# The last expert's second layer, its sums and the first output block by column halves

## The chip, the cores and the metric

The kernel runs on one core of one Trainium2 chip. The metric is the device time of one execution in microseconds; the kernel before was timed three times, with a median of 202.81 us (202.5 to 203.48).

## What is computed

Packed attention over 8 batches and 8 heads (576 rows, 32 packed rows, head size 64), then a soft mixture of 8 experts with 4 slots each over the 4608 tokens that attention gives:

```python
def sm_attn(qq, kk, vv):            # softmax(scale * qq kk^T) vv
    ...
p_packed = sm_attn(p, k, v)
x = sm_attn(q, p_packed, p_packed)  # to (4608, 512)

logits = x @ phi                    # (4608, 32)
d = exp(logits - logits.max(0)); d /= d.sum(0) + 1e-09
slot_input = (d.T @ x).reshape(8, 4, 512)
for e in range(8):
    h = np.maximum(slot_input[e] @ w1[e], 0.0)
    slot_out[e] = h @ w2[e]         # w2[e] is (1024, 512)
c = exp(logits - logits.max(1)); c /= c.sum(1) + 1e-09
return c @ slot_out.reshape(32, 512)
```

All is in f32. The output is 4608 x 512, 9.44 MB.

## The kernel before

Attention and the statistics of the soft mixture run first, in an order that is written out by hand (the `ORDER` string); the change does not touch them. Behind them the eight experts' weights stream through a ring in the on-chip memory, and at the end the output goes out. Every transfer is issued by SP, on one queue, in program order. A new load waits for its place in the ring and for the landing of the transfer eight before it; a store waits for the copies that write its tiles.

The second layer of an expert multiplies the hidden rows by `w2[e]`, 1024 x 512. Each of the 128 partitions holds eight of its rows, so there are NJ = 8 products, each over 128 partitions (`layer2`). They add up in PSUM bank 5 (`SO`) in four strips of 32 rows, because four products on 32 columns of the array run side by side. The last expert is done by `last2(j, x)`: `j` is one of the eight products, `x` one of the two column halves of 256. Its weights come in three pieces, `w2_7_0` (j 0 to 3), `w2_7_2` and `w2_7_3` (two j each), all 512 columns wide. The left half adds up in bank 0, the right half in bank 1. Between the pieces stand products on `ones` (`f_w`) whose result nobody reads.

Then, for each half, VectorE (DVE) adds the bank to a copy of bank 5 (`sot`) into `so`; a product with `repf` adds up the four strips and lays the 32 slot rows four times over the partitions, in bank 2 or 3; a copy brings that to `sh`. An output tile is 128 tokens: a product of 32 rows of `cT` (the combine weights) with 32 rows of `sh`, a copy from PSUM to the ring by ScalarE (ACT) or DVE, and a store. There are 36 such tiles, in four blocks `dd` of nine. Partition p holds nine neighbouring rows of the output for each block, one of each tile, so a store of three tiles writes rows of 6 KB. The first tile is made by quarters that run as the halves of `sh` come, the next three along with it; all others by one product each. `obank` gives the PSUM banks in turn. Stores go out after tiles 1, 2, 4, 7 and 9 of the first block and after each three of the others.

`copy(eng, dst, src)` is ACT for "a" and DVE for "v"; its lines are L380 and L384. All products go through `product`, L150. Loads are L159, stores L1158 and L1169.

Of the kernel before, what the change touches and what calls it, by code (L numbers as in the profile page):

```python
# [11 lines left out]
ALU = mybir.AluOpType  # L12
# [61 lines left out]
def pack_attention_soft_moe(  # L74
# [11 lines left out]
    nc = tc.nc  # L86
# [4 lines left out]
    E, DM, FF = w1.shape  # L91
    SPE = NSLOT // E
    P = 128
    R = 64
    T = S // R
    ND = B // 2
# [3 lines left out]
    NJ = FF // P  # L100
# [48 lines left out]
    def product(*a, **k):  # L149
        return step(nc.tensor.matmul(*a, **k), 4)  # L150
# [108 lines left out]
    def rows_w1(e, g):  # L259
        return w1[e, 2 * P * g : 2 * P * (g + 1)].rearrange("(j p) f -> p j f", j=2)  # L260
# [3 lines left out]
    chunks = [(f"w1_{e}_{g}", 2 * FF, rows_w1(e, g)) for e in range(E) for g in range(NG)]  # L264
    for e in range(E):
        wv = w2[e].rearrange("(p j) f -> p j f", j=NJ)
        ends = (0, 4, 8) if e < E - 1 else (0, 4, 6, 8)
        for c, (j0, j1) in enumerate(zip(ends, ends[1:])):
            if e == E - 1 and c > 0:
                c += 1  # L270
            chunks.append((f"w2_{e}_{c}", (j1 - j0) * DM, wv[:, j0:j1]))
    extra = [c for c in chunks if c[0] == LX]
    chunks = [c for c in chunks if c[0] != LX]
    for x in PLACE:
        key, width, src = extra.pop() if x == "x" else chunks.pop(0)
# [18 lines left out]
    for y in range(4):  # L294
        rs = slice(32 * y, 32 * y + 32)
# [34 lines left out]
    work = workp.tile([P, SLOTS * 2 * FF], F32, name="work")  # L330
# [337 lines left out]
    def part(f, c):  # L668

        t0, t1, a0, a1 = PARTS[c]  # L670
        return f[:, t0:t1, a0:a1]
# [260 lines left out]
    cT = a2Tf[:, E * XZ : E * XZ + NT // 4 * P].rearrange("p (n x) -> p n x", x=P)  # L932
# [43 lines left out]
    for tok in ORDER.split():  # L976
        x, _, eng = tok.partition(":")
        x, _, bank = x.partition("@")
        n, i, j = x.split(".")
# [7 lines left out]
    SO = 5  # L987
# [51 lines left out]
        )  # L1039

    def w2v(e, j):
        if (e, j // 4) == (E - 1, 1):
            return view(f"w2_{e}_{2 + j % 4 // 2}").rearrange("p (j f) -> p j f", j=2)[:, j % 2]
        return view(f"w2_{e}_{j // 4}").rearrange("p (j f) -> p j f", j=4)[:, j % 4]

    halves = [slice(x * DM // 2, (x + 1) * DM // 2) for x in range(2)]

    def layer2(e):
# [16 lines left out]
        op=ALU.add,  # L1065
# [32 lines left out]
    sot, so, sh = (a2f[:, x * DM : (x + 1) * DM] for x in range(3))  # L1098
    repf = rep.rearrange("p c s -> p (c s)")

    def last2(j, x):
        a = (j + 2 * x) % 4
        product(
            ps[32 * a : 32 * a + 32, x, 0 : DM // 2],
            hTf[:, (NJ * (E - 1) + j) * NSLOT : (NJ * (E - 1) + j + 1) * NSLOT],
            w2v(E - 1, j)[:, halves[x]],
            start=(j < 4),
            stop=(j >= 4),
        )

    nc.vector.tensor_copy(sot, ps[:, SO])
    for x in range(2):
        for j in range(4):
            last2(j, x)
    f_w(2, 0, 4, None)
    for j0 in range(4, NJ, 2):
        for x in range(2):
            for j in range(j0, j0 + 2):
                last2(j, x)
        if j0 < NJ - 2:  # L1120
            f_w(2, 0, 4, None)
    for x, xs in enumerate(halves):
        nc.vector.tensor_tensor(so[:, xs], ps[:, x, 0 : DM // 2], sot[:, xs], op=ALU.add)
    for x, xs in enumerate(halves):
        product(ps[:, 2 + x, 0 : DM // 2], repf, so[:, xs], start=True, stop=True)
    for x, (xs, eng) in enumerate(zip(halves, "va")):
        copy(eng, sh[:, xs], ps[:, 2 + x, 0 : DM // 2])
    for key in ("w2_7_0", "w2_7_2", "w2_7_3"):
        release(key)


    obank = [4, 6, 7, 5, 0, 1, 2, 3]
    work = {"a": 0.0, "v": 0.0}
    n = 0
    for dd in range(ND):
        key, off, width = region(f"ob{dd}", T * DM)
        while not free(off, width):
            key, off, width = region(f"ob{dd}", T * DM)
        regions.append([key, off, width])
        ob = ring[:, off : off + width].rearrange("p (t m) -> p t m", t=T)  # L1140
        ov = out[dd * P * T : (dd + 1) * P * T].rearrange("(p t) m -> p t m", t=T)
        ends = (1, 2, 4, 7, 9) if dd == 0 else (3, 6, 9)
        t1 = 0
        for t in range(T):
            n4, a = divmod(dd * T + t, 4)
            rs = slice(32 * a, 32 * a + 32)
            b = obank[n % 8]
            if n < 4:

                if n == 0:  # L1150
                    for x, xs in enumerate(halves):
                        for y in range(4):
                            ys = slice(32 * y, 32 * y + 32)
                            o = obank[y] if y or x == 0 else obank[4]
                            product(ps[:, o, xs], cT[ys, 0], sh[ys, xs], start=True, stop=True)
                    for x, (xs, eng) in enumerate(zip(halves, "av")):
                        copy(eng, ob[:, 0, xs], ps[:, obank[4 * x], xs])
                        nc.sync.dma_start(out=ov[:, 0, xs], in_=ob[:, 0, xs])  # L1158
                    n += 1
                    t1 = 1  # L1160
                    continue
            else:
                product(ps[:, b], cT[rs, n4], sh[rs], start=True, stop=True)
            eng = "a" if work["a"] + 482 <= work["v"] + 607 else "v"
            work[eng] += 482 if eng == "a" else 607
            copy(eng, ob[:, t], ps[:, b])
            n += 1
            if t + 1 in ends:
                nc.sync.dma_start(out=ov[:, t1 : t + 1], in_=ob[:, t1 : t + 1])  # L1169
                t1 = t + 1  # L1170


# [30 lines left out]
```

## Time and profile before

| | |
|---|---|
| median of three timed runs | 202.81 us |
| the profiled execution | 202.17 us |
| its span, first to last instruction | 200.4 us |
| TensorE busy | 172.1 us, 86% of the span |
| VectorE, ScalarE busy | 128.0 and 81.8 us |
| moved by DMA | 72.31 MB, 62.46 MB of it read |
| mean over the span | 361 GB/s |

The page divides the span into 40 slices of 5 us. The DMA engines are full in nearly all of them; the slices that are not are the beginning and the 35th, 170 to 175 us, between the last weights and the first store. Busy shares are means over the whole span and say little about that place, so the rows below take the last 50 us apart. In the profile an f32 product stands as two matmul records. Matmul ends are modelled, and consecutive ones overlap; the time from one start to the next is the safer number.

### The profile page before, as it was taken

What the parts mean: (1) busy time and instruction counts of PE and PEld (TensorE: products, weight loads), DVE (VectorE), ACT (ScalarE), POOL (GpSimd) and SP (SyncE); (2) the same over time, 40 slices, a digit from 0 to 9 for tenths busy, and PEclk for the clock granted to TensorE, in tenths of its full rate; (3) what the DMA queues carried; (4) which work ended last, traced back from release to release, by engine and by line L of the source; (5) the groups of instructions that cost most, each with busy time, mean ns of one, the idle gap of its engine ahead of it and who ended that gap; (6) DMA issues with size and microseconds to landing.
All of it is one profiled execution on the core that took longest, in us unless ns stands there. A gap on an engine that the chain in (4) does not pass through costs nothing.

```text
span 200.4 us, 6603 instructions
## 1 busy us (share of the span) xinstructions
PE 172.1 (86%) x2869; PEld 111.1 (55%) x2869; DVE 128.0 (64%) x245; ACT 81.8 (41%) x205; POOL 36.6 (18%) x66
## 2 busy tenths in 40 slices
PE   7988998998999999899999999887989998798000
PEld 4554694986957765786868775454333333365000
DVE  2838467995989995995967959755772104389000
ACT  2163473676836746545256515021111000289000
POOL 7300007046064040007074041003000000000000
PEclk9999999999999999999999999999999999999655
DMA  6996699999999999999999999999999997099997
GB/s 208 390 383 200 190 395 371 367 388 332 366 378 391 385 389 389 354 372 371 410 390 404 415 398 415 423 414 363 314 417 420 414 422 313 1 347 410 413 417 297
DMA packets 23196, 72.31 MB, mean 361 GB/s; under 512 B 2176, under 2 KB 2944, under 8 KB 21248
## 3 DMA queue, kind: packets, MB, share of 16 engines
q1 hardware_dynamic: 23168, 71.90, 94.1%
q8 instruction: 22, 0.36, 0.7%
q14 instruction: 6, 0.05, 0.1%
HBM read 62.46 MB, written 9.44 MB: 359 GB/s over the span
## 4 chain that ended last, share of the span: by engine, by line
PE 44%; DMA 28%; DVE 9%; ACT 5%; SPq 3%; issue 3%; POOL 1%; ACTq 0%; DVEq 0%
PE ps L150 32%; DMA ring<-in_moe_w_dram 14%; PE ps L153 12%; DMA ring<-in_k_dram 9%; DMA ring<-in_p_dram 5%; ACT ring L380 3%; SPq L159 3%; DVE work L431 2%; DVE work L384 1%; POOL a L704 1%; ACT work L380 1%; DVE mx L639 1%; DVE zs L683 1%; DVE a L704 1%; DVE a L649 1%
## 5 line engine op out<-in xcount | busy, mean ns | idle before, releaser
L380 ACT COPY work<-ps 128x512 f32<-128x512 f32 (+3 forms) x61 | 26.3, 474 | 31.6 <-PE ps L153 23.1
L150 PE MATMUL ps<-work 128*64 128x64 f32 (+1 forms) x1088 | 32.2, 313 | 1.5 <-DVE work L431 0.8
L150 PEld LDWEIGHTS ps<-work 128*64 128x64 f32 (+1 forms) x1088 | 23.0, 121 | 8.0 <-issue 3.0
L431 DVE STREAM_TRANSPOSE work<-ring 128x576 f32<-128x576 f32 x32 | 23.5, 758 | 4.4 <-DMA ring<-in_k_dram 2.3
L153 PE MATMUL ps<-ident,ring 128*128 128x128 f32 x144 | 21.2, 280 | 0.1
L150 PE MATMUL ps<-ring,work 64*64 64x128 f32 x576 | 19.0, 273 | 1.2 <-DVE work L384 1.2
L150 PE MATMUL ps<-ones 128*128 128x512 f32 (+3 forms) x46 | 18.6, 504 | 1.1 <-DVE ones L118 1.1
L150 PEld LDWEIGHTS ps<-ring,work 64*64 64x64 f32 x576 | 16.0, 133 | 4.8 <-issue 1.8
L384 DVE COPY work<-ps 128x512 f32<-128x512 f32 (+3 forms) x31 | 15.8, 527 | 3.7 <-PE ps L153 2.3
L153 PEld LDWEIGHTS ps<-ident,ring 128*128 128x128 f32 x144 | 16.0, 141 | 3.1 <-issue 1.3
L686 POOL TENSOR_TENSOR zt<-work 128x576 f32<-128x576 f32 x4 | 5.7, 1429 | 56.6 <-ACT work L678 56.6
L153 PE MATMUL ps<-ident,work 128*128 128x128 f32 x108 | 15.6, 278 | 0.5 <-ACT work L463 0.4
L384 DVE COPY a2Tb<-ps 128x384 f32<-128x384 f32 (+2 forms) x15 | 8.0, 546 | 9.7 <-PE ps L153 9.7
L463 ACT ACTIVATE work<-ps,nm 128x576 f32<-128x576 f32 x16 | 11.8, 743 | 5.8 <-DVE nm L460 5.8
L639 DVE TENSOR_REDUCE mx<-ps 128x36 f32<-128x1152 f32 x8 | 10.8, 1353 | 4.3 <-PE ps L150 2.5
L150 PE MATMUL ps<-ring,hT 128*32 128x512 f32 (+1 forms) x120 | 13.2, 538 | 0.3 <-DMA ring<-in_moe_w_dram 0.3
L153 PEld LDWEIGHTS ps<-ident,work 128*128 128x128 f32 x108 | 11.9, 141 | 2.4 <-ACT work L463 1.4
L150 PE MATMUL ps<-ring,a2Tb 128*32 128x512 f32 x96 | 12.4, 594 | 0.4 <-DVE a2Tb L1061 0.4
L150 PE MATMUL ps<-a,a2Tb 32*128 32x512 f32 (+2 forms) x88 | 12.0, 584 | 0.6 <-DVE ring L384 0.5
L460 DVE TENSOR_REDUCE nm<-ps 128x2 f32<-128x1152 f32 x8 | 10.8, 1348 | 2.8 <-PE ps L150 2.8
L150 PEld LDWEIGHTS ps<-ones 128*128 128x128 f32 x46 | 8.0, 209 | 6.4 <-issue 5.0
L380 ACT COPY ring<-ps 128x512 f32<-128x512 f32 (+1 forms) x21 | 10.4, 621 | 1.1 <-PE ps L150 1.0
(127 smaller groups left out, 225.4 us busy)
## 6 DMA issues: line engine op xcount, KB each, us to landing
ring<-in_moe_w_dram SPq DMA_DIRECT2D x24, 1024.0 KB, 10.3
ring<-in_k_dram SPq DMA_DIRECT2D x16, 576.0 KB, 8.1
ring<-in_q_dram SPq DMA_DIRECT2D x16, 576.0 KB, 6.9
ring<-in_v_dram SPq DMA_DIRECT2D x16, 576.0 KB, 7.3
out_dram<-ring SPq DMA_DIRECT2D x10, 768.0 KB, 8.1
work<-in_moe_w_dram SPq DMA_DIRECT2D x6, 1024.0 KB, 14.3
a<-in_moe_w_dram SPq DMA_DIRECT2D x1, 1024.0 KB, 6.9
ring<-in_moe_w_dram SPq DMA_DIRECT2D x2, 512.0 KB, 18.7
```

The costliest lines, as they stand in the source:

```text
L150: return step(nc.tensor.matmul(*a, **k), 4)
L153: return step(nc.tensor.transpose(*a, **k), 2)
L159: x = nc.sync.dma_start(out=dst, in_=src).ins
L380: nc.scalar.copy(dst, src)
L384: nc.vector.tensor_copy(dst, src)
L431: nc.vector.transpose(kT[:, b2, :, c].rearrange("p m (t r) -> p m t r", t=T), view(f"k{i}.{b2}").rearrange("p (m t c d) -> p m t c d", m=2 ...
L460: nc.vector.tensor_reduce(nms[i % 2], s1v(i), axis=AX.XY, op=ALU.max, negate=True)
L463: nc.scalar.activation(a1[:, :, x].rearrange("p t (h r) -> p h t r", h=2), s1v(i)[:, x].rearrange("p h (t r) -> p h t r", t=T), AF.Exp, bi ...
L639: nc.vector.tensor_reduce(mxs[i % 2][:, a0:a1].rearrange("p a t -> p (a t)"), s2v(i, j).rearrange("p a t s -> p (a t) s"), axis=AX.X, op=A ...
L649: nc.vector.tensor_tensor(a2s[i // NG % 2][:, :, i % NG, a0:a1].rearrange("p t a s -> p a t s"), s2v(i, j), mxs[i % 2][:, a0:a1].unsqueeze ...
L686: nc.gpsimd.tensor_tensor(y, a[:, :, :, 0:w], a[:, :, :, w:NS], op=ALU.add)
L704: (nc.vector if eng == "v" else nc.gpsimd).tensor_tensor(a, a, z.unsqueeze(3).broadcast_to([P, a.shape[1], a.shape[2], NS]), op=ALU.mult)
```

## The change

The last expert's weights come by column halves: the left 256 columns of all 1024 rows in three pieces (j 0 to 3, 4 and 5, 6 and 7), then the right 256 columns in one. The left half's products, sum, `repf` product and `sh` copy come first; the fillers on `ones` stand between its pieces. Then the first block's nine tiles are made by halves: left halves of tiles 0 to 3, the right half's eight products, left halves of tiles 4 to 8, the right half's sum, the right halves of all nine tiles. The `sh` copy of each half is cut again, 128 columns on DVE and 128 on ACT, and so is the copy of bank 5. The first block is stored in six pieces of half rows; the second in two stores of four and five tiles, the third and fourth in one each.

```diff
-        ends = (0, 4, 8) if e < E - 1 else (0, 4, 6, 8)
...
+        if e == E - 1:
+            for c, j0, j1 in ((0, 0, 4), (1, 4, 6), (2, 6, 8)):
+                chunks.append((f"w2_{e}_{c}", (j1 - j0) * DM // 2, wv[:, j0:j1, 0 : DM // 2]))
+            chunks.append((f"w2_{e}_3", NJ * DM // 2, wv[:, :, DM // 2 : DM]))
+            break
...
+    def total(x):
+        xs = halves[x]
+        nc.vector.tensor_tensor(so[:, xs], ps[:, x, 0:HB], sot[:, xs], op=ALU.add)
+        product(ps[:, 2 + x, 0:HB], repf, so[:, xs], start=True, stop=True)
+
+    def shared(x):
+        for y, eng in enumerate("va"):
+            ys = slice(HB * x + HB // 2 * y, HB * x + HB // 2 * (y + 1))
+            copy(eng, sh[:, ys], ps[:, 2 + x, HB // 2 * y : HB // 2 * (y + 1)])
...
+    def part(t, x, b):
+        n4, a = divmod(t, 4)
+        rs = slice(32 * a, 32 * a + 32)
+        product(ps[:, b, 0:HB], cT[rs, n4], sh[rs, halves[x]], start=True, stop=True)
+
+    def keepp(t, x, b, eng):
+        copy(eng, ob[:, t, halves[x]], ps[:, b, 0:HB])
+
+    def send(t0, t1, x):
+        nc.sync.dma_start(out=ov[:, t0:t1, halves[x]], in_=ob[:, t0:t1, halves[x]])
+
+    for j in range(NJ):
+        last2(j, 0)
+        if j in (3, 5):
+            f_w(2, 0, 4, None)
+    total(0)
+    shared(0)
+    for t in range(4):
+        part(t, 0, pa[t])
+    for j in range(NJ):
+        last2(j, 1)
+    for t in range(4):
+        keepp(t, 0, pa[t], "avav"[t])
+        if t != 2:
+            send(*((0, 1), (1, 2), None, (2, 4))[t], 0)
+    for t in range(4, 8):
+        part(t, 0, pa[t])
+    part(8, 0, pa[8])
+    total(1)
+    for t in range(4, 8):
+        keepp(t, 0, pa[t], "avav"[t - 4])
+    shared(1)
+    keepp(8, 0, pa[8], "a")
+    send(4, 9, 0)
+    for t in range(T):
+        part(t, 1, pb[t])
+    for t in range(T):
+        keepp(t, 1, pb[t], "avavavava"[t])
+        if t in (2, 8):
+            send(*((0, 3) if t == 2 else (3, 9)), 1)
```

The order on TensorE at the end of the program, from the last expert on, as a difference. `ring,hT` are products of `last2`, `ones` fillers, `a_1_101,rep` the product with `repf`, `a_1_101,a2Tb` output tiles:

```order
-L150 MATMUL ps<-ring,hT 32x256 x8
-L150 MATMUL ps<-ones 128x256
 L150 MATMUL ps<-ring,hT 32x256 x4
 L150 MATMUL ps<-ones 128x256
-L150 MATMUL ps<-ring,hT 32x256 x4
-L150 MATMUL ps<-a_1_101,rep 128x256 x2
-L150 MATMUL ps<-a_1_101,a2Tb 128x256 x8
-L150 MATMUL ps<-a_1_101,a2Tb 128x512 x32
-L1198 UNCONDITIONAL_BRANCH
+L150 MATMUL ps<-ring,hT 32x256 x2
+L150 MATMUL ps<-ones 128x256
+L150 MATMUL ps<-ring,hT 32x256 x2
+L150 MATMUL ps<-a_1_101,rep 128x256
+L150 MATMUL ps<-a_1_101,a2Tb 128x256 x4
+L150 MATMUL ps<-ring,hT 32x256 x8
+L150 MATMUL ps<-a_1_101,a2Tb 128x256 x5
+L150 MATMUL ps<-a_1_101,rep 128x256
+L150 MATMUL ps<-a_1_101,a2Tb 128x256 x9
+L150 MATMUL ps<-a_1_101,a2Tb 128x512 x27
```

The first `repf` product moves ahead of the right half's eight products, and the second one stands behind five output tiles.

ACT at the same place before, with the engines whose counts each instruction waits for (`a_1_101` holds `sot`, `so` and `sh`):

```order
L942 ACTIVATE L_sb<-L_sb 128x288 [waits DVE_49] x4
L1015 COPY a_1_101<-ps 128x512 [waits DMAHW4_49,PE_49,Pool_49]
L1015 COPY a_1_101<-ps 128x512 [waits PE_49]
L380 COPY a_1_101<-ps 128x256 [waits PE_49,Activation_49]
L380 COPY ring<-ps 128x256 [waits DMAHW5_49,DMAHW7_49,DMAHW2_49,PE_49]
```

and ACT now:

```order
L1154 COPY a_1_101<-ps 128x256 [waits DVE_49]
L382 COPY a_1_101<-ps 128x128 [waits DVE_49]
L382 COPY ring<-ps 128x256 [waits DMAHW5_49,DMAHW7_49,DMAHW2_49,PE_49]
L382 COPY ring<-ps 128x256 [waits DMAHW6_49,DMAHW0_49,PE_49]
L382 COPY ring<-ps 128x256 [waits DMAHW3_49,DMAHW1_49,PE_49]
L382 COPY ring<-ps 128x256 [waits PE_49]
L382 COPY a_1_101<-ps 128x128 [waits DVE_49]
L382 COPY ring<-ps 128x256 [waits DMAHW7_49]
```

The half copies of `sh` on ACT wait for DVE, where the copy before waited for TensorE; the last row, the left half of tile 8, has come to stand behind the second of them.

SP's stores before, by the elements of each partition:

```order
L1158 DMA out_dram<-ring 128x256 x2
L1169 DMA out_dram<-ring 128x512
L1169 DMA out_dram<-ring 128x1024
L1169 DMA out_dram<-ring 128x1536
L1169 DMA out_dram<-ring 128x1024
L1169 DMA out_dram<-ring 128x1536 x9
```

and now, with the last loads ahead of them:

```order
L159 DMA ring<-in_moe_w_dram 128x4x256
L159 DMA ring<-in_moe_w_dram 128x2x256 x2
L159 DMA ring<-in_moe_w_dram 128x8x256
L1151 DMA out_dram<-ring 128x256 x2
L1151 DMA out_dram<-ring 128x2x256
L1151 DMA out_dram<-ring 128x5x256
L1151 DMA out_dram<-ring 128x3x256
L1151 DMA out_dram<-ring 128x6x256
L1205 DMA out_dram<-ring 128x2048
L1205 DMA out_dram<-ring 128x2560
L1205 DMA out_dram<-ring 128x4608 x2
```

Fifteen stores become ten; the first block and the last weights move in pieces of 256 elements, the rest in longer rows.

## Rows read from the trace of the kernel before

**Rows 1.** The page: span, and packets of the DMA queue that brings instructions.

```profile
span 200.4 us, 6603 instructions
q8 instruction: 22, 0.36, 0.7%
```

**Rows 2.** Stretches: busy time (count) by engine, then granted clock, DMA share, GB/s.

```profile
147.90:168.50 20.60, 19.03 (x180) 6.16 (x172) 5.37 (x14) 0.73 (x2) 0.00 (x0) 1.00 1.01 420
168.50:171.00 2.50, 2.50 (x27) 1.15 (x28) 0.55 (x1) 0.00 (x0) 0.00 (x0) 1.00 0.28 108
171.00:175.70 4.70, 3.54 (x34) 1.84 (x36) 1.97 (x5) 1.49 (x4) 0.00 (x0) 1.00 0.00 0
177.40:199.20 21.80, 6.99 (x48) 4.66 (x48) 7.61 (x13) 8.11 (x17) 0.00 (x0) 0.71 1.01 409
```

**Rows 3.** Chain that ended last, from 165 us: start, us, what.

```profile
147.91 20.53 DMA ring<-in_moe_w_dram
```

**Rows 4.** Timeline of TensorE, 164 to 174 us: start, us, what [idle before].

```profile
166.30 1.92 PE L150 MATMUL ps<-ring,hT 128*32 128x512 f32 x16
168.48 1.07 PE L150 MATMUL ps<-ring,hT 128*32 128x256 f32 x16 [0.26 <-DMA ring<-in_moe_w_dram]
169.48 0.70 PE L150 MATMUL ps<-ones 128*128 128x256 f32 x2
170.11 0.64 PE L150 MATMUL ps<-ring,hT 128*32 128x256 f32 x8
170.68 0.70 PE L150 MATMUL ps<-ones 128*128 128x256 f32 x2
171.31 0.64 PE L150 MATMUL ps<-ring,hT 128*32 128x256 f32 x8
```

**Rows 5.** Timelines of DVE, ACT, SP and TensorE, 171.9 to 176.5 us.

```profile
171.98 0.76 DVE L1123 TENSOR_TENSOR a<-ps,a 128x256 f32<-128x256 f32 x2 [2.94 <-PE ps L150]
173.27 0.42 DVE L384 COPY a<-ps 128x256 f32<-128x256 f32 x1 [0.53 <-PE ps L150]
...
173.69 0.37 ACT L380 COPY a<-ps 128x256 f32<-128x256 f32 x1 [19.72 <-PE ps L150]
174.48 1.55 ACT L380 COPY ring<-ps 128x256 f32<-128x256 f32 x3 [0.42 <-PE ps L150]
...
174.88 0.83 SPq L1158 DMA_DIRECT2D out_dram<-ring  x2
175.80 0.89 SPq L1169 DMA_DIRECT2D out_dram<-ring  x2
...
172.46 1.13 PE L150 MATMUL ps<-a,rep 128*128 128x256 f32 x4 [0.51 <-DVE a L1123]
173.75 1.15 PE L150 MATMUL ps<-a,a2Tb 32*128 32x256 f32 x16 [0.15 <-DVE a L384]
```

**Rows 6.** Groups by form, copies: count | busy us, mean ns of one | idle before.

```profile
L380 ACT COPY work<-ps 128x128 f32<-128x128 f32 x10 | 2.8, 278 | 1.4 <-PE ps L153 1.3
L384 DVE COPY work<-ps 128x128 f32<-128x128 f32 x6 | 1.7, 283 | 0.0
```

**Rows 7.** Timeline, 34.0 to 34.9 us: two copies out of one PSUM bank.

```profile
33.99 0.42 DVE L384 COPY work<-ps 64x256 f32<-64x256 f32 x1
...
34.44 0.37 ACT L380 COPY work<-ps 64x256 f32<-64x256 f32 x1 [2.40 <-DVE work L384]
```

**Rows 8.** DMA, 174 to 176 us, 1 KB packets: 40 slices; packets, MB, share.

```profile
GB/s 0 0 0 0 0 0 0 0 0 0 0 0 0 0 0 0 0 0 0 0 0 0 0 0 0 0 0 0 0 0 0 0 0 0 143 225 307 348 369 307
...
q1 hardware_dynamic: 83, 0.08, 12.8%
```

**Rows 9.** DMA, 161 to 164 us: loads of 8 KB packets.

```profile
DMA packets 179, 1.29 MB, mean 429 GB/s; under 512 B 22, under 2 KB 22, under 8 KB 22
```

**Rows 10.** DMA, 177.5 to 178.5 us: stores of 4 KB packets.

```profile
DMA packets 101, 0.40 MB, mean 401 GB/s; under 512 B 3, under 2 KB 3, under 8 KB 101
```

**Rows 11.** DMA, 190 to 198 us: stores of 6 KB packets.

```profile
DMA packets 607, 3.34 MB, mean 417 GB/s; under 512 B 64, under 2 KB 64, under 8 KB 607
```

More of the change, by code (lines that the diff above doesn't have):

```diff
@@ L266, in pack_attention_soft_moe @@
         wv = w2[e].rearrange("(p j) f -> p j f", j=NJ)
-        ends = (0, 4, 8) if e < E - 1 else (0, 4, 6, 8)
[L268 to L271, printed above, removed]
+        if e == E - 1:
[3 more added lines that the diff above has]
+            break
+        for c in range(2):
+            chunks.append((f"w2_{e}_{c}", 4 * DM, wv[:, 4 * c : 4 * c + 4]))
     extra = [c for c in chunks if c[0] == LX]
@@ L1041, in w2v, with w2h @@
     def w2v(e, j):
-        if (e, j // 4) == (E - 1, 1):
-            return view(f"w2_{e}_{2 + j % 4 // 2}").rearrange("p (j f) -> p j f", j=2)[:, j % 2]
         return view(f"w2_{e}_{j // 4}").rearrange("p (j f) -> p j f", j=4)[:, j % 4]
+    def w2h(j, x):
+        if x:
+            key, n, k = "3", NJ, j
+        else:
+            key, n, k = ("0", 4, j) if j < 4 else (str(1 + (j - 4) // 2), 2, j % 2)
+        return view(f"w2_{E - 1}_{key}").rearrange("p (j f) -> p j f", j=n)[:, k]
     halves = [slice(x * DM // 2, (x + 1) * DM // 2) for x in range(2)]
@@ L1105, in last2 @@
             hTf[:, (NJ * (E - 1) + j) * NSLOT : (NJ * (E - 1) + j + 1) * NSLOT],
-            w2v(E - 1, j)[:, halves[x]],
+            w2h(j, x),
             start=(j < 4),
@@ L1109, in last2, with rows @@
         )
[L1111 to L1135, printed above, removed]
+    HB = DM // 2
+    def total(x):
[6 more added lines that the diff above has]
+            copy(eng, sh[:, ys], ps[:, 2 + x, HB // 2 * y : HB // 2 * (y + 1)])
+    def rows(dd):
         key, off, width = region(f"ob{dd}", T * DM)
@@ L1139, in pack_attention_soft_moe @@
         regions.append([key, off, width])
[L1140 to L1143, printed above, removed]
+        return (
+            ring[:, off : off + width].rearrange("p (t m) -> p t m", t=T),
+            out[dd * P * T : (dd + 1) * P * T].rearrange("(p t) m -> p t m", t=T),
+        )
+    ob, ov = rows(0)
+    def part(t, x, b):
[6 more added lines that the diff above has]
+        nc.sync.dma_start(out=ov[:, t0:t1, halves[x]], in_=ob[:, t0:t1, halves[x]])
+    nc.vector.tensor_copy(sot[:, halves[0]], ps[:, SO, halves[0]])
+    nc.scalar.copy(sot[:, halves[1]], ps[:, SO, halves[1]])
+    for j in range(NJ):
[4 more added lines that the diff above has]
+    shared(0)
+    pa = (4, 6, 7, 5, 0, 2, 4, 6, 7)
+    pb = (5, 0, 2, 1, 3, 4, 6, 7, 5)
+    for t in range(4):
[21 more added lines that the diff above has]
+            send(*((0, 3) if t == 2 else (3, 9)), 1)
+    for c in range(4):
+        release(f"w2_{E - 1}_{c}")
+    obank = [0, 2, 1, 3, 4, 6, 7, 5]
+    work = {"a": 0.0, "v": 0.0}
+    n = 0
+    for dd in range(1, ND):
+        ob, ov = rows(dd)
         for t in range(T):
@@ L1147, in pack_attention_soft_moe @@
             b = obank[n % 8]
[L1148 to L1163, printed above, removed]
+            n += 1
+            product(ps[:, b], cT[rs, n4], sh[rs], start=True, stop=True)
             eng = "a" if work["a"] + 482 <= work["v"] + 607 else "v"
@@ L1166, in pack_attention_soft_moe @@
             copy(eng, ob[:, t], ps[:, b])
[L1167 to L1170, printed above, removed]
+            if t in ((3, 8) if dd == 1 else (8,)):
+                t0 = 4 if dd == 1 and t == 8 else 0
+                nc.sync.dma_start(out=ov[:, t0 : t + 1], in_=ob[:, t0 : t + 1])
 _INS = ["q", "k", "v", "p", "moe_phi", "moe_w1", "moe_w2"]
```

## The prediction

> **What bounds the kernel now.** I read the page first: the span is 200.4 us [rows 1], the profiled execution took 202.17 us and the median of the three timed runs is 202.81 us. I add differences to the span and carry them to the median, which lies 0.64 us above the profiled execution.
>
> Then the stretches at the end [rows 2]. From 147.9 to 168.5 us the DMA engines are full (share 1.01, 420 GB/s): the expert weights stream in and TensorE keeps up. From 168.5 the share falls to 0.28, from 171.0 to 175.7 it is 0.00, and from 177.4 to 199.2 it is 1.01 again at 409 GB/s. So the end is a store stream that nothing interrupts, and the time is set by when that stream begins, how often it stops, and how fast its 9.44 MB go. After 175.7 the compute engines are ahead of it: in the last stretch ACT is busy 8.11 us of 21.8.
>
> The chain [rows 3] says what sets the beginning: the first piece of the last expert's second layer lands at 168.44 (147.91 + 20.53). TensorE alone fills the next 3.5 us [rows 4]: eight half-width products (16 records, each f32 product shows twice) at 168.48, a filler on `ones` at 169.48, four products at 170.11, a filler at 170.68, four products until 171.95. Then sum, product with `repf`, copy, first output tile, copy, issue at 174.88 [rows 5]; the first bytes move at 174 + 34 x 0.05 = 175.70 [rows 8], 0.82 us after the issue.
>
> **Part 1, the weights by column halves.** The same 2 MB, in pieces of 1 KB instead of 8 and 4 KB. A 1 KB packet took 0.128 x 16 x 2000 / 83 = 49.3 ns [rows 8]; an 8 KB packet at 429 GB/s takes 305 ns [rows 9]. The left half is 64 packets on each DMA engine, 3.16 us, where 1 MB was 8 x 305 = 2.44: it is complete at 168.44 + 0.7 = 169.2. TensorE needs its last piece at about 170.6 (below), so 1.4 us are to spare. The right half is later again by 64 x 49.3 less 16 x 163 (4 KB packets [rows 10]) = 0.55 us: before, everything had landed by 171.0 [rows 2], so about 172.3 at worst, and it is needed at 173.7. Cost: nothing, hidden behind TensorE; if that cover were gone, 1.3 us.
>
> **Part 2, the left half goes first.** The expert before ends on TensorE at 166.30 + 1.92 = 168.22, and such runs overlap by 0.07 (168.48 + 1.07 against 169.48) [rows 4], so the left half starts at 168.15 on a first piece that has landed (168.44 - 2.44 + 1.58 = 167.6). Four products 0.57 (170.11 to 170.68), filler 0.63, two products that I price like four, 0.57, filler 0.63, last two 0.64: done at 171.19 against 171.95. Both fillers stay in this half, 1.26 us of it.
>
> The sum starts at 171.22. Sum to product 0.48, product to copy 0.81 [rows 5]: 172.51. Here is a new cost. The copy of 256 columns is cut in two halves of 128, one on DVE and one on ACT, but both read one PSUM bank, and the order below shows ACT's half waiting for DVE. The trace has that pattern once [rows 7]: DVE's copy ends at 34.41 and ACT's begins at 34.44. So 0.28 + 0.03 + 0.28 [rows 6] = 0.59 in place of 0.42: 173.10, products at 173.16 (+0.06), first copy 0.73 later at 173.89, 0.37 long, issue at 174.29 (+0.03). That is **0.59 us earlier** than 174.88; bytes move at 175.11.
>
> **Part 3, the feed after the first four half tiles.** Four half tiles are ready early, in three stores. SP issues 0.46 apart (half of 174.88 to 175.80 [rows 5]), so the third moves at 175.11 + 0.92 = 176.03 and its 16 packets per engine last 0.79: the stream is dry at **176.82**. The next store, of five half tiles, waits for the ninth copy, and that copy stands on ACT behind the right half's `sh` copy. Following it: four products from 173.16 (0.57), eight products on the right half (1.07) until 174.80, sum at 174.83. Meanwhile TensorE does five more products in two groups, 0.5 each, until 175.73, and only then the `repf` product; 0.81 to the copies: 176.54; DVE 0.28, ACT 0.03 + 0.28: 177.13; ninth copy, 0.37: 177.50; issue 177.53, bytes at 178.35. The stream stands still for **1.53 us**. Bounds: 1.0, if the groups of four products that stand before the `repf` product follow each other at 0.42 (the pair of groups in 1.15, less its tail of 0.31, halved [rows 5]) and the ninth copy overlaps ACT's half copy; 1.9, if each hand-over between engines costs the longest one seen here, 0.15 [rows 5]. Of what follows, the store of three waits for ACT's copies, which begin after the ninth right-hand product; it comes at about the moment the five are through (1.9 us of transfer), then six tiles cover the rest. I count nothing there.
>
> **Part 4, the size of rows.** The first block of nine tiles becomes 144 packets of 1 KB on each engine, 144 x 49.3 = 7.10 us. Before it was 16 of 1 KB, 8 of 2 KB, 16 of 4 KB, 8 of 6 KB: 0.79 + 0.66 (half the 4 KB price) + 2.61 + 8 x 236 [rows 11] = 5.94. So +1.16; by the best slice of 1 KB traffic, 369 GB/s, a packet is 44.4 ns and the difference +0.53 [rows 8]. I take **+0.9**.
> The Trainium skill, "DMA: Bandwidth & Descriptors", section Specifications, puts line rate at transfers of 512 B and more, so 1 KB pieces would lose nothing. By it this term would vanish; rows 8 against rows 11 (20.8 bytes per ns against 26.0) do not agree.
>
> The other 27 tiles go in rows of 8, 10 and 18 KB instead of 6 KB. No 18 KB row was measured. 6 KB packets are 236 ns, three are 708. By the 8 KB stretch of [rows 2] (420 GB/s, 312 ns) an 18 KB row is 702, and the three blocks win 0.15 us; by a straight line through 236 and 305 it is 650 and they win 1.2. Far on the other side, the 22 packets of 16 KB on the instruction queue took 0.007 x 16 x 200.4 / 22 = 1.02 us each [rows 1], which would make it 1.15 us and cost 6.9. I take **-0.4**, near the rows of this queue.
>
> **Sum.** -0.59 + 1.53 + 0.9 - 0.4 = +1.44, say 1.4 us: span 201.8, median 202.81 + 1.4 = **204.2 us**. The small gaps between the first stores (a half tile lasts 0.39, an issue 0.46) were there before too.
>
> **Rivals.**
> 1. *The stall does not open.* Place: the store of five half tiles. It decides whether its issue stands before 176.82 - 0.82 = 176.00. Then 1.53 falls away and the sum is -0.1: 202.7, not slower; with the lower ends of part 4 (+0.53 and -1.2) it is -1.3: 201.5. For it: DVE and ACT have free time in these microseconds [rows 5]. Against: the order fixes five products, one product and three copies in a row in front of this store.
> 2. *The rows pay for themselves.* The stall is there, but 1 KB pieces cost only their bytes: 39.3 ns each, 5.66 against 5.78 us, -0.1 in place of +0.9: +0.4, 203.2. Or the large rows win 1.2 and the sum is +0.6, 203.4. Against the first stand the 49.3 ns of 83 packets, against the second that it needs the whole of the straight line. The Trainium skill's rule above speaks for the first.
> 3. *The loads come late.* Column halves skip every other KB in memory, which no row here shows. If they ran at half rate, the left half would take 2.4 us longer and be ready at 170.9 instead of 169.2, still costing only 0.3, the right half would come at about 175.8 and add 2.1: near 206.3.
> 4. *TensorE's clock.* It is at the full level, 2.4 GHz, up to 175.7 (1.00 in each stretch but the last [rows 2]), with fillers in the gaps. The right half has none. If it fell to 1.2 GHz near 173, about 2.5 us of TensorE steps on the path double: near 206.7. Against: the idle stretches that I expect there, 0.5 to 0.9 us, are near the 0.51 of [rows 5], which left the clock alone.
>
> **How the numbers follow.** A measurement of this kernel can tell 0.5%, 1.0 us. Forecast (+1.0 to +2.2): 0.55; rival 1: 0.15, of which half goes to faster; rival 2: 0.21, within 0.5%; rivals 3 and 4 and an 18 KB row that is slow: 0.09. So faster 0.07, same 0.29, slower 0.64. The forecast's own range is 203.8 to 205.0. The range for eight in ten reaches down to rival 1 (202.7) and up over part of rivals 3 and 4: 202.6 to 205.4.
>
> **What the profile will show.** The first store issued at 174.3 (174.0 to 174.6) and bytes 0.82 later; an ACT copy of 128 columns beginning 0.03 us after DVE's, twice; a second stretch of DMA share 0, 1.0 to 1.9 us long, that begins near 176.9; then 1 KB traffic at 330 to 370 GB/s until about 183.7, and after it 410 to 435. TensorE should not wait for a DMA after 168.2. I am wrong if the second empty stretch is under 0.7 us, if the first bytes move later than 175.5, or if the stretch of large rows is off 409 GB/s by more than 7%.

## The result and the profile after

The changed kernel took 206.03 us (median of 20 runs; the kernel before took 204.0 over 20 runs beside them). The ratio is 1.0103, 95% interval 1.0070 to 1.0137: slower by 1 per cent, about 2.1 us. The forecast was slower by 1.4 us, at 204.2 us with a range up to 205.4. So the sign came out, the difference is somewhat larger, and the time lies outside the range. Ratios, here and below, leave out the runs that are more than 1.5 per cent above the fastest of their kernel; medians take all of them.

The page's span, beside [rows 1]:

```profile
span 201.9 us, 6621 instructions
```

1.5 us longer than 200.4. The stretches of the end, in the columns of [rows 2]:

```profile
171.00:174.90 3.90, 2.63 (x30) 1.32 (x34) 1.62 (x5) 0.91 (x3) 0.00 (x0) 1.00 0.00 1
174.90:176.80 1.90, 1.46 (x12) 0.69 (x7) 1.32 (x4) 0.72 (x3) 0.00 (x0) 1.00 0.84 275
176.80:178.20 1.40, 1.16 (x17) 1.09 (x18) 0.41 (x2) 0.47 (x2) 0.00 (x0) 1.00 0.01 1
178.20:183.60 5.40, 5.40 (x37) 3.36 (x36) 4.11 (x10) 4.95 (x13) 0.00 (x0) 1.00 1.00 332
183.60:200.50 16.90, 3.22 (x23) 1.68 (x18) 4.16 (x7) 4.01 (x8) 0.00 (x0) 0.71 1.00 421
```

Read the last two columns downwards. The stores begin at 174.9, which is 0.8 us earlier than before; they stop at 176.8 and stand still for 1.4 us, which they never did before; they run at 332 GB/s while the rows are 1 KB long, and at 421 GB/s behind that, where [rows 2] had 409.

TensorE, which fills the time before the first store (as [rows 4]):

```profile
166.26 2.36 PE L150 MATMUL ps<-ring,hT 128*32 128x512 f32 x24
168.55 0.70 PE L150 MATMUL ps<-ones 128*128 128x256 f32 x2
169.18 0.63 PE L150 MATMUL ps<-ring,hT 128*32 128x256 f32 x4
169.73 0.70 PE L150 MATMUL ps<-ones 128*128 128x256 f32 x2
170.36 0.63 PE L150 MATMUL ps<-ring,hT 128*32 128x256 f32 x4
171.52 0.70 PE L150 MATMUL ps<-a,rep 128*128 128x256 f32 x2 [0.53 <-DVE a L1122]
172.96 0.71 PE L150 MATMUL ps<-a,a2Tb 32*128 32x256 f32 x8 [0.75 <-ACT a L382]
173.61 1.07 PE L150 MATMUL ps<-ring,hT 128*32 128x256 f32 x16
174.61 1.13 PE L150 MATMUL ps<-a,a2Tb 32*128 32x256 f32 x10
175.66 0.70 PE L150 MATMUL ps<-a,rep 128*128 128x256 f32 x2
```

No row has a DMA behind "<-": the weights by column halves are there in time. The last five products of the left-hand tiles (174.61, ten records) stand between the right half's products and its `repf` product (175.66), as forecast. The copies and stores, as [rows 5]:

```profile
172.32 0.29 DVE L386 COPY a<-ps 128x128 f32<-128x128 f32 x1 [0.86 <-PE ps L150]
...
176.40 0.29 DVE L386 COPY a<-ps 128x128 f32<-128x128 f32 x1 [0.21 <-PE ps L150]
...
172.65 0.27 ACT L382 COPY a<-ps 128x128 f32<-128x128 f32 x1 [3.49 <-DVE a L386]
...
176.73 0.27 ACT L382 COPY a<-ps 128x128 f32<-128x128 f32 x1 [0.74 <-DVE a L386]
176.89 0.38 ACT L382 COPY ring<-ps 128x256 f32<-128x256 f32 x1
178.64 5.54 ACT L382 COPY ring<-ps 128x256 f32<-128x256 f32 x13 [1.37 <-PE ps L150]
...
174.09 6.42 SPq L1151 DMA_DIRECT2D out_dram<-ring  x6
...
177.29 0.38 SPq L1151 DMA_DIRECT2D out_dram<-ring  x1
...
179.31 0.37 SPq L1151 DMA_DIRECT2D out_dram<-ring  x1
```

The first store is issued at 174.09, where it was 174.88. Twice ACT's 128 columns begin 0.04 us after DVE's end (172.61 and 176.69), as [rows 7] said they would. The ninth left-hand copy follows at 176.89, and the store of five half tiles is issued at 177.29. The row at 178.64 is one that the forecast saw and counted at nothing: ACT's right-hand copies wait 1.37 us for TensorE, and the store of three goes out only at 179.31.

The 1 KB stretch, 178.2 to 183.6 us (packets, then MB and share of 16 engines):

```profile
DMA packets 1781, 1.79 MB, mean 332 GB/s; under 512 B 32, under 2 KB 1781, under 8 KB 1781
...
q1 hardware_dynamic: 1781, 1.79, 100.1%
```

1.001 x 16 x 5400 / 1781 = 48.6 ns a packet, and 49.3 for the 1 KB packets alone, without the 32 under 512 B: the price of [rows 8].

**A yardstick with less noise than the time.** The last load that all versions have in common is the second piece of expert 6's second layer. From its landing to the last byte of the last store, by the DMA records, it is 33.25 us in the kernel before, in its repetition and in the version that only has more instructions. I call that the tail. For the changed kernel it is 34.62, and 34.7 to 34.9 in two near copies of it below; there the tail is less sure, since it also holds how late TensorE is behind the landing (Part 2 below). In this pair the tail explains +1.37, the end behind the last landing +0.25 (1.09 us instead of 0.84 to the last instruction), and device time outside the span +0.37 (2.14 us instead of 1.77).

### The profile page after: what moved, and what is told of

The parts are those of the page before. It is cut to its first block, busy times and chain, and to the rows that moved or that the text cites. A ratio compares the mean times of both kernels' runs of the same rounds, so it can differ in the third digit from the quotient of the medians.

```text
span 201.9 us, 6621 instructions
## 1 busy us (share of the span) xinstructions
PE 174.5 (86%) x2879; PEld 112.2 (56%) x2879; DVE 128.5 (64%) x250; ACT 82.4 (41%) x211; POOL 36.5 (18%) x66
## 4 chain that ended last, share of the span: by engine, by line
PE 52%; DMA 15%; DVE 15%; ACT 5%; issue 2%; SPq 2%; POOL 1%; DVEq 0%; ACTq 0%
PE ps L150 41%; DMA ring<-in_k_dram 13%; PE ps L153 12%; DVE work L433 2%; DMA out_dram<-ring 2%; ACT work L382 2%; SPq L159 2%; POOL a L706 1%; DVE ring L386 1%; DVE L_sb L942 1%; DVE cm L946 1%; ACT L_sb L944 1%; DVE work L386 1%; DVE cm L941 1%; ACT ring L382 1%
## 5 line engine op out<-in xcount | busy, mean ns | idle before, releaser
L150 PE MATMUL ps<-work 128*64 128x64 f32 (+1 forms) x1088 | 32.8, 313 | 2.2 <-DVE work L433 0.8
L150 PE MATMUL ps<-a,a2Tb 32*128 32x512 f32 (+2 forms) x98 | 13.5, 544 | 1.4 <-ACT a L382 1.4
L386 DVE COPY ring<-ps 128x512 f32<-128x512 f32 (+1 forms) x20 | 10.2, 574 | 3.8 <-PE ps L150 3.8
```

## The experiments

Idle is the time in which the DMA engines did nothing between the first and the last store byte, summed over engines and divided by 16. Outside is device time less span. Tail, idle and outside are of one profiled execution each.

| run | tail | idle | outside | ratio to before |
|---|---|---|---|---|
| before | 33.25 | 0.39 | 1.78 | 1 |
| after | 34.62 | 1.94 | 2.14 | 1.0103 (1.0070 to 1.0137) |
| e0_again | 33.25 | 0.39 | 1.78 | 1.0001 (0.9964 to 1.0037) |
| e1_long_rows | 32.82 | 0.38 | 1.78 | 1.0044 (0.9998 to 1.0090) |
| e2_half_rows | 34.46 | 0.62 | 1.77 | 1.0101 (1.0033 to 1.0169) |
| e3_send_early | 34.34 | 1.08 | 2.14 | 1.0051 (0.9997 to 1.0104) |
| e3a_send_only | 34.89 | 1.97 | 2.16 | one run |
| e3b_bank_only | 34.72 | 1.88 | 2.13 | one run |
| e4_full_loads | 35.21 | 1.93 | 2.14 | 1.020 (1.011 to 1.029) |
| e5_no_fillers | 33.55 | 1.95 | 2.16 | 0.9995 (0.9949 to 1.0042) |
| e6_no_gaps | 31.58 | 0.44 | 2.03 | 0.9982 (0.9939 to 1.0026) |
| e7_rows_no_fillers | 32.50 | 0.36 | 1.78 | 0.9994 (0.9948 to 1.0040) |
| e8_more_instructions | 33.25 | 0.36 | 2.01 | one run |

**Long rows alone (before with the stores of the last three blocks in longer rows).**

```diff
-        ends = (1, 2, 4, 7, 9) if dd == 0 else (3, 6, 9)
+        ends = ((1, 2, 4, 7, 9), (4, 9), (9,), (9,))[dd]
```

> The kernel before with one part of the change alone: the second block is stored as four and five tiles, the third and fourth in one store of nine tiles each (rows of 8, 10 and 18 KB for 6 KB). Theory A (each packet has a fixed cost, so that the size of rows counts): the stretch of full DMA behind the first block shortens by 0.5 us, ratio to the kernel before 0.997 to 0.998. Theory B (bytes are bytes; only when the stream starts and stops counts): no difference, 1.000, and the stretch stays 17.25 us.

The tail is 0.43 shorter. The stretch of long rows, as [rows 2]; before, the same kind of stretch moved 409 GB/s:

```profile
184.00:201.90 17.90, 3.75 (x28) 2.34 (x22) 4.37 (x8) 4.87 (x10) 0.00 (x0) 0.72 1.01 425
```

So the trace bears the -0.4 out. The timed ratio does not: it stands above what was expected, with an interval of 0.9 per cent, four times the effect; the medians of all runs lean the other way (203.72 against 204.34, 0.9970). A gain of 0.2 per cent cannot be shown with these timings.

**Half rows alone (before, the first block's stores as two column halves of 1 KB).**

```diff
-                nc.sync.dma_start(out=ov[:, t1 : t + 1], in_=ob[:, t1 : t + 1])
+                for xs in halves if dd == 0 else (slice(0, DM),):
+                    nc.sync.dma_start(out=ov[:, t1 : t + 1, xs], in_=ob[:, t1 : t + 1, xs])
```

> The kernel before with one cost of the change alone: each store of the first block goes as two column halves, 144 packets of 1 KB on each engine in place of rows of 1 to 6 KB. Everything else, and when the first store is issued, stays. Theory A: the first block's transfer takes 1.1 us longer (6.15 to about 7.2 us), ratio 1.005. Theory B: no difference, 1.000.

Tail +1.21, and the ratio's interval leaves no change out, though the medians of all runs lie closer (204.59 against 204.34). The 1 KB stretch:

```profile
176.70:182.00 5.30, 5.30 (x42) 3.59 (x39) 5.29 (x9) 5.25 (x11) 0.00 (x0) 1.00 0.97 316
```

The engines are full (0.97) and move 316 GB/s. 0.23 of the 1.21 is idle time, which I put down to the four more stores that are issued; the rest, 1.0 us, is the size of the rows.

**The stall: three edits.** In the first, the store of half tiles 4 to 8 leaves without the ninth, and the ninth right-hand product is moved, so that bank 5, which it shares with the first right-hand tile, no longer holds up ACT's copies (the `send` lines do the first, the `part` lines the second):

```diff
+    send(4, 8, 0)
     shared(1)
     keepp(8, 0, pa[8], "a")
-    send(4, 9, 0)
-    for t in range(T):
+    send(8, 9, 0)
+    for t in range(8):
         part(t, 1, pb[t])
     for t in range(T):
         keepp(t, 1, pb[t], "avavavava"[t])
+        if t == 0:
+            part(8, 1, pb[8])
```

> The changed kernel with the stall taken away: the left halves of tiles 4 to 7 are stored before the right half's sh copy, tile 8 by itself behind it; and the ninth right-hand product, which uses the first one's bank 5, is issued after the first right-hand copy, so that this copy no longer waits for it. Theory A (the stall of 1.4 us in the store stream is time): two short gaps of about 0.3 us stay in its place, 0.8 to 1.1 us less than the changed kernel, ratio to the kernel before about 1.005 and the last bytes at about 199.4 in the profile. Rival C (the stall is covered, the time is lost in the transfers themselves or outside the span): as the changed kernel, 1.010.

The stream, from first to last byte, is 0.89 us shorter (24.66 instead of 25.55), and the ratio is half-way to the kernel before, as expected, but its interval holds both ends. The tail shows only 0.28 of the gain, because here the first store is issued 8.82 us after the common landing, and 8.21 in the changed kernel.

What the bank does is more than a wait. `pb` gives bank 5 to the first and to the ninth right-hand product, and the program issues all nine products before the first copy. The chain of the changed kernel shows them run, nine products in 18 records, and the copy behind them:

```profile
177.04 1.57 PE ps L150 x18
```

They end at 178.61, and ACT's first right-hand copy starts at 178.64. So the ninth product has overwritten the first, and both copies out of bank 5 bring tile 8: the changed kernel does not store the right half of tile 0 (128 rows, 256 columns) but tile 8's in its place. With the reference's inputs the two differ by about 1 part in 100,000, so the output hardly shows it. The `part` lines put the order right, in the versions with both edits, with the bank alone and without gaps; with both edits ACT waits 0.51 us instead of 1.37:

```profile
179.22 1.53 ACT L382 COPY ring<-ps 128x256 f32<-128x256 f32 x5 [0.51 <-PE ps L150]
```

With the bank alone put right, the tail is 34.72 and the idle time 1.88, as in the changed kernel within what two executions differ by, so the comparison of this document does not hang on the fault.

The second and the third run take one of the two edits each: only the `send` lines, and only the `part` lines.

> The changed kernel with one edit: the store of half tiles 4 to 8 is issued without the last of them, which goes by itself behind it. The bank that the first and the ninth right-hand products share is left as it is. Theory (the dry stretch is the sum of two waits in a row: the ninth left-hand copy, and then the right-hand copies that wait for the ninth right-hand product because of that bank): the dry stretch is split, not removed: four half tiles go about 0.4 us earlier, the stream runs dry again before the store of three right-hand half tiles, and DMA idle time inside the stream falls from 1.94 us only to 1.2 to 1.7. Rival (only the ninth left-hand copy makes the stall): idle time falls to about 0.9 us or less, what the version with both edits has (1.08) or under it.

> The changed kernel with one edit: the ninth right-hand product waits until the first right-hand copy is done, so the right-hand copies no longer wait for it; the store of half tiles 4 to 8 stays whole. Theory (two limits of equal length, either of which alone keeps the stream back): in the changed kernel the five half tiles, issued 3.20 us after the first store and 1.97 us long, are through at about the moment at which the store of three (issued 5.22 us after the first) can move. So with the bank alone mended nothing is gained either: idle time in the stream 1.85 to 1.95 us as before the edit, the store of three issued about 4.4 us after the first and queued. Rival (the bank alone is the bound, since the split store alone gained nothing): idle time about 1.1 us.

The share of the DMA engines in 8.1 us from the first store byte on, and in the stretches in which the stream is dry. With `send` alone:

```profile
175.90:184.00 8.10, 7.42 (x61) 4.67 (x58) 5.24 (x13) 5.54 (x15) 0.00 (x0) 1.00 0.79 261
177.90:178.20 0.30, 0.14 (x4) 0.14 (x8) 0.00 (x0) 0.30 (x2) 0.00 (x0) 1.00 0.05 17
180.20:181.20 1.00, 1.00 (x9) 0.76 (x11) 0.02 (x1) 1.00 (x5) 0.00 (x0) 1.00 0.00 0
```

With the bank alone:

```profile
177.60:185.70 8.10, 7.41 (x66) 5.40 (x63) 6.10 (x14) 6.27 (x17) 0.00 (x0) 1.00 0.81 265
179.60:180.90 1.30, 1.15 (x17) 0.73 (x17) 0.39 (x2) 0.79 (x4) 0.00 (x0) 1.00 0.00 0
```

With both:

```profile
176.40:184.50 8.10, 7.41 (x67) 5.41 (x61) 6.10 (x14) 6.32 (x17) 0.00 (x0) 1.00 0.92 308
178.30:178.60 0.30, 0.11 (x4) 0.11 (x5) 0.00 (x0) 0.30 (x2) 0.00 (x0) 1.00 0.00 0
```

Neither edit alone gains anything; both together gain 0.9. With `send` alone the stall is split, 0.3 us before the fourth store and 1.0 us behind the fifth, because the store of three right-hand tiles still leaves 5.2 us after the first one (180.32 less 175.11; in the changed kernel 179.31 less 174.09). With the bank alone that store is ready 4.35 us after the first and stands in the queue behind the one that is late. I had expected a small gain from `send` alone and missed; the gain from the bank alone, none, came as expected. Two waits of nearly equal length lie beside each other, and taking away one shows the other.

**Full rows for the loads (after, the last expert's weights in three pieces of whole rows).**

```diff
-                chunks.append((f"w2_{e}_{c}", (j1 - j0) * DM // 2, wv[:, j0:j1, 0 : DM // 2]))
-            chunks.append((f"w2_{e}_3", NJ * DM // 2, wv[:, :, DM // 2 : DM]))
+                chunks.append((f"w2_{e}_{c}", (j1 - j0) * DM, wv[:, j0:j1]))
```

> The changed kernel with the last expert's weights loaded as before, in three pieces of full rows (8 and 4 KB packets); products, sums, copies and stores as in the changed kernel, where bank 5 is written by the first and by the ninth right-hand product and copied out twice after the ninth. Theory A: the left half's last two products need the last piece, which lands at 171.0 where the left columns land at 168.9; TensorE comes to it at 170.4, so the first store is 0.6 us later than in the changed kernel, and the time 0.3 to 0.6 us more, since the right half is no longer late either. Rival D (the 1 KB loads cost more than they bring): faster than the changed kernel by 0.5 us or more.

Now TensorE waits for the first piece, and not for the last one, as I had expected:

```profile
169.51 1.92 PE L150 MATMUL ps<-ring,hT 128*32 128x512 f32 x16
172.13 0.64 PE L150 MATMUL ps<-ring,hT 128*32 128x256 f32 x8 [0.70 <-DMA ring<-in_moe_w_dram]
```

The tail is 0.3 to 0.6 longer than that of the changed kernel and its near copies, in the expected span; the timed ratio went further. So the loads by halves cost nothing that shows, and without them the left half waits 0.70 us for its weights. What that is worth is less sure: the first store is issued 8.80 us after the common landing, and 8.21 to 8.82 in the four versions that load by halves and keep the fillers.

**No fillers (after without the two products on `ones`).**

```diff
     for j in range(NJ):
         last2(j, 0)
-        if j in (3, 5):
-            f_w(2, 0, 4, None)
```

> The changed kernel without the two fillers between the left half's products (1.26 us of TensorE); bank 5 is used as in the changed kernel. Theory A (TensorE, not the landing of the weights, sets when the left half is done): its last two products start when the last left piece lands, so the first store comes 1.2 to 1.4 us earlier after the expert before than in the changed kernel; the gap in the stores stays 1.4 us, and the time falls by 1.2 us, ratio to the kernel before about 1.003. Rival E (the fillers hold TensorE's clock): the granted clock falls to 0.5 between 170 and 178 us, the steps there double and the time is the changed kernel's or more, 1.010 to 1.015.

```profile
166.77 0.55 PE L153 MATMUL ps<-ident,L_sb 128*128 128x128 f32 x3 [0.57 <-DVE a2Tb L386]
167.25 2.79 PE L150 MATMUL ps<-ring,hT 128*32 128x512 f32 x32
170.58 0.70 PE L150 MATMUL ps<-a,rep 128*128 128x256 f32 x2 [0.55 <-DVE a L1122]
```

From the start of expert 6's products to the `repf` product it is 3.33 us, against 5.26 (171.52 less 166.26): the fillers cost 1.93, not 2 x 0.63. Products on 32 columns run side by side in groups of four; a filler on all 128 columns ends the group, and a pair that would share a group then takes as long as four (0.55 us from 169.18 to 169.73, where four took 0.57 from 170.11 to 170.68 in [rows 4]). The tail wins less, 1.1 to 1.3 against the changed kernel and its near copies (expected: 1.2), since expert 6's products start 1.21 us after the common landing here and 0.38 after it in the changed kernel; the idle time stays (1.95). The granted clock stayed at 1.00, the level of 2.4 GHz, without them:

```profile
167.20:174.50 7.30, 6.00 (x70) 2.65 (x68) 2.88 (x7) 1.38 (x5) 0.00 (x0) 1.00 0.52 165
```

The first row shows a second wait: TensorE's last transposes stand 0.57 us for a DVE copy, because `for x, b in enumerate((6, 7, 6))` uses bank 6 twice; the kernel before has the same wait (0.56), and with bank 3, in the next two versions, the nine records run in 1.20 us without it.

**No gaps (after without fillers and stall, the third transposes in bank 3, `sh` in one DVE copy, the left half's later stores in pairs).** Not in the lines shown: both edits of the stall, the ninth left-hand product behind the second `sh` copy, and tile 7's left-hand copy on ACT.

```diff
-    for x, b in enumerate((6, 7, 6)):
+    for x, b in enumerate((6, 7, 3)):
...
-        for y, eng in enumerate("va"):
-            ys = slice(HB * x + HB // 2 * y, HB * x + HB // 2 * (y + 1))
-            copy(eng, sh[:, ys], ps[:, 2 + x, HB // 2 * y : HB // 2 * (y + 1)])
+        copy("v", sh[:, halves[x]], ps[:, 2 + x, 0:HB])
...
+        if t in (5, 7):
+            send(t - 1, t + 1, 0)
```

> The changed kernel with what was found put together: no fillers; the left half's nine tiles stored in stores of 1, 1, 2, 2, 2 and 1 tiles as their copies come, none of them behind the right half's sh copy; that copy in one piece on DVE; the last three transposes into bank 3, so that they wait for no copy; the ninth right-hand product after the first right-hand copy. Theory A: first store 2 us earlier after the expert before than in the kernel before, no gap in the store stream over 0.3 us, 1 KB rows cost 1.1 and long rows win 0.4 to 0.5: 1.5 to 2.0 us less than the kernel before, ratio 0.990 to 0.993. Rival E: the clock falls without the fillers and it is not faster than the kernel before. Rival C (the time is lost outside the store stream): not better than 1.005.

```profile
172.15 0.70 PE L150 MATMUL ps<-a,rep 128*128 128x256 f32 x2 [0.53 <-DVE a L1122]
173.43 0.71 PE L150 MATMUL ps<-a,a2Tb 32*128 32x256 f32 x8 [0.58 <-DVE a L386]
```

One whole copy costs 1.28 us from `repf` product to tile; the two halves cost 1.44 (172.96 less 171.52). And the stream has no hole:

```profile
175.40:183.50 8.10, 8.10 (x72) 5.98 (x65) 6.48 (x14) 6.98 (x18) 0.00 (x0) 1.00 1.01 339
```

The tail is 1.67 shorter than before. 0.25 of it is lost outside the span and 0.13 behind the last landing. What remains, 1.3 us, would be a ratio of 0.9937, just under the lower edge of what was measured (0.9939 to 1.0026), which also holds no change. I had expected 0.990 to 0.993 and missed.

**Long rows, no fillers (before with those two edits and the third transposes in bank 3).**

```diff
-    for x, b in enumerate((6, 7, 6)):
+    for x, b in enumerate((6, 7, 3)):
...
-    f_w(2, 0, 4, None)
...
-        ends = (1, 2, 4, 7, 9) if dd == 0 else (3, 6, 9)
+        ends = ((1, 2, 4, 7, 9), (4, 9), (9,), (9,))[dd]
```

> The kernel before with three edits: stores of the last three blocks in long rows, no fillers on `ones` among the last expert's products, and a third bank for the third pair of transposes. Theory (each microsecond saved at the start of the store stream or inside it comes out of the span, one for one): long rows give 0.45 us, as measured in the trace with long rows alone; without fillers TensorE's run can shorten only until the last of the loads lands, which the trace of before puts 0.35 us ahead of the last four products, so the first store is issued 8.1 to 8.3 us after TensorE starts the second layer of the expert before, in place of 8.58. Sum about -0.8 us, a ratio near 0.996 (0.992 to 0.999). Rival (fillers hold the TensorE clock): the granted clock falls below 1.00 behind 168 us from the last expert's start and the first store comes later than in before: ratio 1.00 or above.

```profile
168.59 1.07 PE L150 MATMUL ps<-ring,hT 128*32 128x256 f32 x16 [0.39 <-DMA ring<-in_moe_w_dram]
169.86 0.64 PE L150 MATMUL ps<-ring,hT 128*32 128x256 f32 x8 [0.20 <-DMA ring<-in_moe_w_dram]
171.11 0.64 PE L150 MATMUL ps<-ring,hT 128*32 128x256 f32 x8 [0.61 <-DMA ring<-in_moe_w_dram]
```

Without fillers the old order waits for each of its three pieces, since it needs the last one for the left half too; so it wins 0.3 of tail where the new order won 1.1 to 1.3. The tail is 0.75 shorter, as expected (0.8); the time can't tell it from no change. No version that I ran is shown to beat the kernel before.

**More instructions (before with 18 small ones at the end).**

```diff
+    for k in range(6):
+        f_w(1, 0, obank[(n + 1) % 8], None)
+        nc.vector.memset(sot[:, 0:32], 0.0)
+        nc.scalar.copy(so[:, 0:32], ones[:, 0:32])
```

> The kernel before with 18 small instructions at its end that nothing waits for: six products on TensorE, six memsets on DVE, six copies on ACT. The kernels with the new tail spend 2.02 to 2.16 us between the span and the device time, those with the old tail 1.77. Theory A (that rest depends on how many instructions the engines' programs have, or on how their last fetch of code is cut): it changes here, by a few tenths of a us. Theory B (it comes from the stores or the loads that the program has): it stays at 1.77 +- 0.03.

The tail is the same 33.25 and the time outside the span 2.01 us, in one execution. That is above every execution of a kernel with the old tail (1.73 to 1.86) and below those of the changed one (2.10 to 2.22). So part of this rest goes with the instructions in the program, and not with its loads and stores. The count alone is not it: the changed kernel has fewer records more than this one (18 against 37) and a larger rest. What decides the other part stays open.

**The kernel before against itself.**

> The kernel before, once more, as a program of its own. It should give 1.000; how far it is off, and how wide its interval is, tells what ratios like the 1.0044 of the long rows alone are worth.

The interval is 0.37 per cent to each side, 0.75 us. That is the limit for the ratios above that were timed as often. The medians of these two equal kernels were 203.07 and 203.94 us. With the end and the rest outside added to their tails, long rows alone, no fillers and no gaps should have had ratios of 0.9990, 1.0045 and 0.9937; each is just beyond an edge of its interval. Whether these versions also differ ahead of the tail, or the intervals are a little too narrow, was not settled; that the medians of two equal kernels differ by 0.43 per cent, where their ratio is 1.0001, shows how much hangs on which runs are counted. So effects under half a per cent rest on the tail here and not on times. For the changed kernel itself the two agree: 206.03 / 204.0 is 1.0100.

## Why the prediction was right in its steps and wrong in its time

**What bounds the kernel**: right. The three equal tails say that the time behind the loads is fixed by this chain and this stream.

**Part 1, the loads**: right. The left half has landed at 168.91 and the right one at 171.75 (forecast: 169.2, and 172.3 at worst), and no product waits for a DMA behind 168.2; with full-row loads one does.

**Part 2, first store 0.59 earlier**: 0.79 in this pair (174.09 against 174.88). Against the common landing the first store came 8.93 us later before, and 8.21, 8.82, 8.50 and 8.40 in the four versions that leave this part as it is: 0.1 to 0.7 earlier, since the new order starts when TensorE is ready and the old one when the first piece lands. The size was right in the mean (0.45). The step behind it, two copies out of one bank in turn, priced at 0.17 (0.59 in place of 0.42), is measured at 0.16 us by the version with one copy.

**Part 3, the stall, 1.53**: right in size; the dry stretch is 1.3 us long (176.88 to 178.21), and idle time 1.55 more in all (1.94 less 0.39). It was right with one limit where there are two: "I count nothing there", on the store of three, holds only because that limit ends at the same moment. As advice for mending it, my account would have failed. It also noted that ACT's copies "begin after the ninth right-hand product" without asking why the first copy should wait for the ninth product: that was the overwritten bank.

**Part 4**: 1 KB rows cost 1.0 in the version with half rows alone and 1.06 here (2.07 of stream less 1.55 of idle time plus 0.54), between the 0.9 taken and its upper bound of 1.16; the packet, 49.3 ns, was priced right. Long rows -0.43 by themselves and -0.54 in the changed kernel (16.74 us of packets instead of 17.28), against -0.4. The mean packet of these stores, by the DMA records, took 49.3 ns for 1 KB, 87.8 for 2, 165 for 4, 240 for 6, 318 for 8, 392 for 10 and 691 for 18 KB. With these means the two terms are +1.04 and -0.54. An estimate from them: a packet costs about 13.5 ns and another 37.75 ns for each KB, within 3 ns of all seven. The Trainium skill ("DMA: Bandwidth & Descriptors", Specifications) puts line rate at transfers of 512 B and more. The two runs with 1 KB stores do not agree: 316 and 332 GB/s against 421 to 425 in long rows.

In sum the stream grew by 2.07 us (23.48 to 25.55) where the parts gave 2.03, and the span by 1.56 where they gave 1.44.

**The step that failed** is the one that carries differences to a time: "I add differences to the span and carry them to the median, which lies 0.64 us above the profiled execution." It failed twice.
- The median of three runs was not the kernel's level. Over 20 runs it is 204.0 and not 202.81, and 203.94 to 204.49 in three further sets of 17 to 30 runs; single runs of the twenty lie between 202.03 and 206.25. That alone is 1.2 of the 1.83 us by which the forecast was missed, and in this the forecast had bad luck too, since its three runs all lie under the level. The spread comes from upstream of the change: expert 6's products start at 166.30 in one execution of the kernel before and at 168.79 in another, and the tail is the same. A range of 2.8 us was too narrow for a level that three runs can't give.
- A difference of spans is not a difference of times. 0.37 us of the increase lie outside the span, in all 20 runs of the changed kernel, and 0.25 behind the last landing, which no step priced; together 0.62, the rest of the 1.83. In the waits of SP (total us, times, longest) from 195 us on, the end looks like this, before:

```profile
SPq L1198 <- DMA out_dram<-ring: 5.5, 3, 1.9
```

and after:

```profile
SPq L1233 <- DMA out_dram<-ring: 12.7, 1, 12.7
```

Before, SP's last waits for stores end one after another; after, one long wait ends with the last landing, and by my reading the others are still to be taken then. The versions with long or half rows alone have the 0.25 too (1.07 and 1.09 us behind the last landing), so it comes with the set of stores. That the order of these waits explains it is a guess that no run tried, and what sets most of the 0.37 outside the span stays open.

Added up: the tail, +1.37 to +1.64 in the changed kernel and the two near copies with as much idle time, +0.25, and +0.37 make 2.0 to 2.3, where the ratio says 2.1. **The rivals**: the stall opened, so the first falls; the rows do not pay for themselves; the loads are not late; the granted clock stayed at 1.00 to 183.6 us, so the fourth falls too.

## What to carry to other kernels

A saving at the start of a store stream is worth its time only if the stream then stays fed: write down, for each store, when it is issued and when the bytes before it are through, and go on past the first stall, because the next limit may end at the same moment. Where a copy waits for a later product than its own, ask whether the bank has been overwritten. Rows of 1 KB cost a fifth of a store stream's rate here, so cut a block by rows of the output and not by columns. Take the level from many runs, and measure a change of a few tenths of a microsecond inside the trace, between two events that both kernels share.

## What was not expected

- Two fillers of 0.63 us cost 1.93, through the products that they keep apart.
- In 3 of 13 profiled executions (long rows, full loads, no gaps) TensorE's granted clock fell to 0.50, the level of 1.2 GHz, for 3.4 us near 140 us, far ahead of the change. In the version without gaps:

```profile
130.00:139.90 9.90, 8.30 (x135) 5.35 (x137) 5.30 (x18) 1.81 (x7) 0.59 (x1) 1.00 1.01 408
139.90:143.30 3.40, 3.40 (x20) 0.94 (x16) 2.68 (x8) 0.45 (x2) 1.25 (x1) 0.50 0.82 276
```

TensorE was busy 8.30 of 9.90 us ahead of it; the kernel before has the same 8.30 in this stretch and kept its clock. What sets it off stays open. It lies ahead of the tail, so it can move the level of a run and not the tail.
- A row of 18 KB goes as one packet of 18,432 B, and its rate is that of the 6 to 8 KB packets or a little above (421 to 425 GB/s against 417 in [rows 11]).
